# Two attention blocks on one core: GpSimd's shifts over four blocks instead of three, the third score bank lent at any time, and a semaphore that holds GpSimd back behind VectorE's shifts and copies of V

## The chip, the cores and the metric

One core of a Trainium2 chip runs the whole program. The metric is device time in microseconds (us), and less is better. Of the engines, TensorE is called PE, VectorE DVE, ScalarE ACT, GpSimd POOL and SyncE SP, as in the profile. PE does matrix products into PSUM (eight banks of 128 partitions by 512 float32 each), ACT does exponentials, DVE and GpSimd do elementwise work, SP issues DMAs.

## The reference, cut to what matters

Both halves have one input of 2048 rows and 512 columns, 32 heads of width 16, and an output projection. Half A is linear attention (cheap); half B is full softmax attention, which is nearly all of the work.

```python
    def _A_ref(x, wqkv, wo):
        ...
        phi = lambda t: jnp.where(t > 0, t + 1, jnp.exp(t)) + 1e-6
        pq, pk = phi(q), phi(k)
        kv = jnp.einsum("bhsd,bhse->bhde", pk, v)
        ...
    def _B_ref(x, wqkv, wo):
        ...
        scores = jnp.einsum("bhqd,bhkd->bhqk", q, k) * scale
        p = _softmax(scores, axis=-1)
        o = jnp.einsum("bhqk,bhkd->bhqd", p, v)
        return (lambda x, *d: x.transpose(*d))(o, 0, 2, 1, 3).reshape(B, S, D) @ wo
```

The two results stand side by side in the output, 2048 by 1024.

## The kernel before

**The unit of work is a block**: 128 keys by 512 queries of one head. There are 32 units (head groups, query stretches and the even or odd heads of a group), each of 64 blocks for four heads, 2048 blocks in all. Each block is one matmul of K and Q into one PSUM bank (`qk`, L863), an exponential, and one or more matmuls of the exponentials with V that add into the bank `pPV` (L1224). V carries a column of ones, so the same product gives the softmax's denominator.

**The exponential is made in one of two ways.** On the ACT way, PE fills two or three banks of the tile `pS` and ACT takes the exponential of all of them in one instruction into `PT` (L1095). `pS` has two slots, of three and two banks (`ABL = (3, 2)`), filled in turn; each further bank makes an instruction longer, and there are fewer of them. On the D way, DVE turns a bank of scores into 16-bit integers that, read as float16, are a coarse exponential (tile `DI`, L970). To make it finer, the same integers are shifted by a constant twice (tile `DJ`, L1166, `k` of 1 and 2), and PE multiplies all three with three copies of V of different weights (`VV`, `k` of 0, 1, 2). So a block of the D way costs DVE one pass over PSUM, GpSimd two shifts, and PE three products with V instead of one. The shifts are done for a group of `DG = 3` blocks at a time, 1536 columns, two instructions to a group, into one of `NDJ = 8` buffers. They run on GpSimd; where GpSimd's planned backlog is over `LM` beyond DVE's, one goes to DVE.

**What sets the order.** A planner in Python runs when the program is built. It keeps a planned time for each engine (`T`), a list of candidates with durations and priorities, and always takes the one that can start first. The order in which it takes them becomes each engine's fixed instruction stream; `Sched.add` notes for each instruction what it must wait for by semaphore. No engine can deviate from this order on the chip. `fill_act_cand` fills a slot of `pS` and, on the way, up to two D blocks into free D banks (`d_pick`); `fill_d_cand` fills a D block alone; `shift_cand` places a shift; `pv_cand` places the products with V; `job_cand` places the projections, half A and the V copies. How many blocks go each way is not set by a number: it falls out of how soon ACT, DVE and GpSimd are free in the plan.

**Banks.** PSUM holds five banks of `pS`, one of `pPV`, two of `pD` (the D banks). The third bank of the large slot can be lent to the D way: then ACT's instruction of that slot takes two banks. `want_lend` decides it; before the change it is lent mainly while a projection or a half A job holds one of the D banks.

**V copies.** For the first head group, DVE itself makes the weighted copies of V (`v4_job`, eight instructions of 544 columns); later ones are made by GpSimd.

**End.** In the last unit no D block is begun once fewer than `DEND = 12` blocks are left; then follow the last exponentials (split in two halves), the last products with V, the division by the denominator, the output projection and the last stores.

The names above are local functions of one large function. Here are those that the change touches:

## Time and profile before

| | |
|---|---|
| time, median of 3 runs | 683.81 us (683.69 to 686.09) |
| the profiled execution | 684.12 us, of which the span of its instructions is 682.4 us |
| PE busy | 653.9 us (96%) |
| ACT busy | 669.0 us (98%) |
| GpSimd (POOL) busy | 622.1 us (91%) |
| DVE busy | 582.6 us (85%) |
| granted clock of TensorE, mean | 0.997 |

The busy time of PE is a poor guide, because its matmuls are pipelined, their ends are modelled, and an instruction that waits with its weights loaded hides in the row of the weight loads. The share of ACT and GpSimd can be taken nearer to the letter, apart from one point: ACT's and DVE's instructions overlap by a few tenths of a microsecond, so that the mean duration of one is longer than the distance between the starts of two. Where a rate matters, it is taken from start to start.

### The profile page before, as it was taken

The page shows a single profiled execution, that of the slowest core. Times are in us where ns is not written, and L with a number is a line of the kernel's source. Part 1 is how long each engine was busy: PE and PEld are TensorE (multiplying, and loading weights), DVE is VectorE, ACT ScalarE, POOL GpSimd, SP SyncE. Part 2 cuts the span into 40 slices and gives each one's busy share as a digit, 9 for nine tenths or more (in the row PEclk, how much of TensorE's full clock was granted, in tenths as well). Part 3 has the DMA queues.
Part 4 walks back from the last instruction along what each step waited for, and adds up shares of the span by engine and source line. Part 5 has one row for each costly group of instructions (what it writes and reads, how often), then busy time and mean ns, then how long its engine had stood idle before and what let it go on. Part 6 is the DMA issues. An engine that isn't in the chain of part 4 may idle for free.

```text
span 682.4 us, 19594 instructions
## 1 busy us (share of the span) xinstructions
PE 653.9 (96%) x8530; PEld 209.9 (31%) x8530; DVE 582.6 (85%) x937; ACT 669.0 (98%) x706; POOL 622.1 (91%) x470
## 2 busy tenths in 40 slices
PE   8999999999999999999999999999999999999997
PEld 4323333222323333332322233222332222322223
DVE  5878898999789988868999898888888998898983
ACT  5999999999999999999999999999999999999997
POOL 6698999999699999999999999999999999999894
PEclk9999999999999999999999998999999999999999
DMA  9400012011101201130111000111010110001111
GB/s 207 103 2 2 17 16 35 10 31 23 34 2 33 33 17 17 22 82 11 24 25 33 24 18 18 24 47 25 18 36 13 33 32 25 9 17 33 47 41 35
DMA packets 55418, 21.76 MB, mean 32 GB/s; under 512 B 45600, under 2 KB 55328, under 8 KB 55328
## 3 DMA queue, kind: packets, MB, share of 16 engines
q1 hardware_dynamic: 54128, 20.07, 13.4%
q8 instruction: 68, 1.11, 0.7%
q10 hardware_dynamic: 1200, 0.39, 0.2%
q14 instruction: 22, 0.18, 0.1%
HBM read 4.19 MB, written 4.19 MB: 12 GB/s over the span
## 4 chain that ended last, share of the span: by engine, by line
ACT 87%; POOL 7%; PE 3%; DVE 2%; DMA 1%; issue 0%; ACTq 0%
ACT PT L1095 85%; POOL DJ L1166 6%; ACT pD L683 1%; DVE DI L970 1%; PE pS L863 1%; DMA xTb<-in_B_x_dram 1%; ACT pS L683 1%; PE pD L535 1%; PE pPV L1224 1%; PE pS L535 1%; PE pS L654 0%; POOL XN L1359 0%; ACT KV L539 0%; POOL VV L671 0%; DVE DJ L1166 0%
## 5 line engine op out<-in xcount | busy, mean ns | idle before, releaser
L1095 ACT ACTIVATE PT<-pS 128x1024 f16<-128x1024 f32 (+1 forms) x666 | 660.5, 1353 | 2.6 <-PE pS L863 1.8
L1166 POOL TENSOR_SCALAR DJ<-DI 128x1536 int16<-128x1536 int16 (+1 forms) x391 | 579.5, 1483 | 48.0 <-DVE DI L970 21.6
L970 DVE TENSOR_SCALAR DI<-pD 128x512 uint16<-128x512 f32 (+1 forms) x456 | 315.2, 705 | 48.4 <-PE pD L863 42.8
L863 PE MATMUL pS<-QT,KM 32*128 32x512 bf16 x1573 | 261.5, 385 | 21.3 <-ACT PT L1095 15.0
L1224 PE MATMUL pPV<-PT,VV 128*17 128x512 f16 (+1 forms) x1420 | 244.0, 378 | 0.5 <-DVE OT L1354 0.5
L1224 PE MATMUL pPV<-DJ,VV 128*17 128x512 f16 (+1 forms) x1256 | 231.9, 379 | 0.7 <-POOL DJ L1166 0.5
L863 PE MATMUL pD<-QT,KM 32*128 32x512 bf16 x475 | 168.5, 385 | 0.3 <-DVE PQT L684 0.3
L863 PEld LDWEIGHTS pS<-QT,KM 32*128 32x128 bf16 x1573 | 64.3, 91 | 278.0 <-ACT PT L1095 260.3
L1224 PE MATMUL pPV<-DI,VV 128*17 128x512 f16 (+1 forms) x628 | 148.3, 379 | 0.5 <-DVE OT L1354 0.4
L970 DVE TENSOR_SCALAR DI<-pS 128x512 uint16<-128x512 f32 x153 | 104.1, 681 | 8.0 <-PE pS L863 4.4
L1224 PEld LDWEIGHTS pPV<-PT,VV 128*17 128x17 bf16 x1420 | 49.8, 88 | 44.0 <-issue 38.1
L1224 PEld LDWEIGHTS pPV<-DJ,VV 128*17 128x17 bf16 x1256 | 47.9, 88 | 47.2 <-issue 35.6
L863 PEld LDWEIGHTS pD<-QT,KM 32*128 32x128 bf16 x475 | 39.7, 91 | 9.3 <-issue 4.1
L1224 PEld LDWEIGHTS pPV<-DI,VV 128*17 128x17 bf16 x628 | 31.2, 88 | 22.4 <-issue 18.4
L1166 DVE TENSOR_SCALAR DJ<-DI 128x1536 int16<-128x1536 int16 x29 | 28.3, 977 | 0.0
L535 PE MATMUL pD<-xTb,Wb 128*32 128x512 bf16 (+1 forms) x368 | 26.7, 379 | 0.0
L535 PE MATMUL pD<-Wa,xTa 128*32 128x256 bf16 x672 | 26.4, 275 | 0.0
L1354 DVE STREAM_TRANSPOSE OT<-pPV 128x512 f32<-128x512 f32 x31 | 22.0, 708 | 0.7 <-PE pPV L1224 0.6
L1359 POOL TENSOR_TENSOR XN<-OT,ZRA 128x256 bf16<-128x256 f32 x31 | 19.5, 630 | 1.2
L683 ACT ACTIVATE pD<-pD 128x512 f32<-128x512 f32 x22 | 19.6, 893 | 0.0
L671 POOL TENSOR_SCALAR VV<-VV 128x544 bf16<-128x544 bf16 x24 | 17.3, 723 | 0.9
L535 PEld LDWEIGHTS pD<-Wa,xTa 128*32 128x32 bf16 x672 | 15.4, 96 | 8.7 <-issue 5.4
(109 smaller groups left out, 392.3 us busy)
## 6 DMA issues: line engine op xcount, KB each, us to landing
out_dram<-KV SPq DMA_DIRECT2D x31, 128.0 KB, 1.7
Wa<-in_A_wqkv_dram SPq DMA_DIRECT2D x3, 512.0 KB, 4.2
KM<-KR SPq DMA_DIRECT2D x96, 16.0 KB, 1.8
Wb<-in_B_wqkv_dram SPq DMA_DIRECT2D x2, 384.0 KB, 4.6
Wb<-in_B_wqkv_dram SPq DMA_DIRECT2D x1, 512.0 KB, 4.4
Wa<-in_A_wo_dram SPq DMA_DIRECT2D x1, 512.0 KB, 4.5
Wb<-in_B_wo_dram SPq DMA_DIRECT2D x1, 512.0 KB, 3.8
xTa<-in_A_x_dram SPq DMA_TRANSPOSE x24, 3.4
```

Of the source, the lines that this page charges most:

```text
L535: ins = e.matmul(out[32 * g:32 * g + 32], lhsT=lhsT[:, 32 * g:32 * g + 32], rhs=rhs, start=start, stop=stop, tile_position=(0, 32 * g))
L671: st.append((lane, 0.74 if lane == "dve" else VVT, f_op(lane, lambda e, k=k: e.tensor_scalar(vv(k), vv(0), SW[k], 0.0, op0=ALU.mult, op1=A ...
L683: ex = lambda bk: sch.add("act", lambda e: e.activation(x(bk), x(bk), ACTF.Exp), reads=[bk[3]], writes=[bk[3]])
L863: return e.matmul(dst, lhsT=KM[32 * g:32 * g + 32, Gp % 2, e_, j * 128:(j + 1) * 128], rhs=QT[32 * g:32 * g + 32, Gp % 2, c * 512:(c + 1) ...
L970: sch.add("dve", lambda e: e.tensor_scalar(DI.bitcast(U16)[:, buf, i * 512:(i + n) * 512], f32v(DBANK[bi], 512 * n), EB, IMAX, op0=ALU.add ...
L1095: sch.add("act", lambda e: e.activation(PT[:, row, c0:c0 + w], SCR[sl][:, 0:w], ACTF.Exp, scale=SC / ESC), reads=skeys(sl)[:len(bl)], writ ...
L1166: sch.add(ln, lambda e: e.tensor_scalar(J, I, 1.0, float(SH[k]), op0=ALU.mult, op1=ALU.add), reads=[("DI", buf, i) for i in range(n)], wri ...
L1224: sch.add("pe", lambda e: e.matmul(dst[32 * g:32 * g + 17, 0:n], lhsT=VV[:, Gp % 2, k, j, 17 * h:17 * h + 17], rhs=P[:, q0:q0 + n], start= ...
L1354: sch.add("dve", lambda e: e.transpose(OT[:, 0, :], PVb[:, 0:512]), reads=[("PV", g) for g in range(4)], writes=[("OT", 0)])
L1359: mul = f_op("pool" if XNP else "dve", lambda e: e.tensor_tensor(xn[:, :, 16 * e_:16 * e_ + 16], o[:, :, 0:16], zr.unsqueeze(2).broadcast_ ...
```

## The change

Seven edits go together, and since the planner sets the order, every engine's stream is a new one.

1. A group has four blocks instead of three (`DG` 4, four buffers of `DI` instead of six, six of `DJ` instead of eight), so a shift is 2048 columns wide.
2. A shift or a copy of V that DVE makes is put on a list `hold`, and the next instruction given to GpSimd waits for it. The plan has DVE wait for the end of GpSimd's planned instruction first, prices the shift itself at 0.45 and the copy at 0.27 in place of 0.40 + 0.0003 a column and 0.74, and puts GpSimd's time behind it.
3. The third bank is lent whenever no D bank is free and neither DVE's nor GpSimd's planned backlog is over a bound (`want_lend`), and with a third bank on loan a D bank that a job holds keeps it lent.
4. Numbers that were one for the whole run (how early a D block is filled, when products with V get precedence, GpSimd's allowed backlog, and two more) are now chosen by stretches of 45 us of the plan from five sets (`MODES`), by the seeds that also shift the due times of the projections and of half A.
5. A job whose last step was GpSimd's counts as ready 0.8 later (`JM`); `PVW` goes from 0.3 to 0; the planner's weights for how busy PE is are changed.
6. The first projections are made by matmuls of 128 columns of weights instead of four of 32 (`first_units`).
7. The plan's start times are changed by up to 0.25, GpSimd's from 16.0 to 8.4.

```diff
+        if lane == "pool" and self.hold:
+            extra_deps = list(extra_deps) + self.hold
+            self.hold = []
...
-    DG = 3
-    NDG = 6
-    NDJ = 8
+    DG = 4
+    NDG = 4
+    NDJ = 6
...
+    MODES = ((0.8, 36, 0.7, 0.2, 9.0), (1.2, 36, 0.7, 0.2, 9.0), (0.8, 48, 0.9, 0.2, 10.5), (1.2, 28, 0.7, 0.1, 9.0), (1.0, 36, 0.55, 0.35, 8.0))
...
+    DSH = 0.45
...
-                        ins = mm4(e, bk[0][:, bk[2] + o0:bk[2] + o0 + n], Wb[:, cc, kind * 512:kind * 512 + 128], xTb[:, cc, c0:c0 + n], cc == 0, cc == 3)
+                        ins = e.matmul(bk[0][:, bk[2]:bk[2] + n], lhsT=Wb[:, cc, kind * 512:kind * 512 + 128], rhs=xTb[:, cc, c0:c0 + n], start=(cc == 0), stop=(cc == 3))
...
+                if lane == "dve":
+                    def alone(bk, cp=cp):
+                        sch.hold.append(cp(bk))
+                        sch.hold[-1].x = 0.27
+                    alone.kind = "x"
+                    st.append(("dve", 0.27, alone))
+                else:
+                    st.append((lane, VVT, cp))
...
         def want_lend(t_):
             nh = sum(1 for i in range(ND) if held.get(i))
-            if LD == 3:
+            if LD == 1:
                 return nh >= 1
-            if LD == 4:
-                return nh >= 2
-            if d_backlog(t_) > LB:
+            free = sum(1 for x in dfree if x is not None and x <= t_ + 0.1)
+            if LD == 2 and sum(1 for i in range(len(dfree)) if held.get(i)) > sum(lent):
+                return True
+            if free:
                 return False
...
-            return False
+            return d_backlog(t_) <= LB and p_backlog(t_) <= PB5
...
-            dp, dd = POOLT(w), 0.40 + w * 0.0003
             sp, sd = max(T["pool"], vis("dve", t_), jfree[jb]), max(T["dve"], t_, jfree[jb])
+            dp, dd = POOLT(w), DSH + max(0.0, T["pool"] - sd)
...
+                if ln == "dve":
+                    T["pool"] = max(T["pool"], vis("dve", en_))
...
+                op = sch.add(ln, lambda e: e.tensor_scalar(J, I, 1.0, float(SH[k]), op0=ALU.mult, op1=ALU.add),
+                             reads=[("DI", buf, i) for i in range(n)], writes=[("DJ", jb)])
+                if ln == "dve":
+                    sch.hold.append(op)
+                    op.x = DSH
```

What the new plan contains, counted in the two programs:

| | before | after |
|---|---|---|
| ACT, exponentials of two banks (1024 columns) | 579 | 581 |
| ACT, exponentials of three banks (1536) | 86 | 78 |
| ACT, exponentials of one bank (512) | 1 | 0 |
| ACT, the two last ones, columns each | 768 | 512 |
| blocks by the ACT way | 1420 | 1398 |
| blocks by the D way | 628 | 650 |
| DVE, `DI` of one bank / of two banks | 590 / 19 | 626 / 12 |
| GpSimd, full shifts | 389 of 1536 | 288 of 2048 |
| GpSimd, short shifts | 2 of 512 | 2 of 1024 |
| DVE, shifts | 29 of 1536 | 36 of 2048 |
| GpSimd's shifts that wait for a semaphore of PE | 27 | 92 |

**ACT, from its first exponential on.** `PT<-pS` of 1024 columns takes two banks of scores, of 1536 three. Before:

```order
L571 ACTIVATE QT<-pD 128x256
L1095 ACTIVATE PT<-pS 128x1024 x14
L1095 ACTIVATE PT<-pS 128x1536
L1095 ACTIVATE PT<-pS 128x1024
L1095 ACTIVATE PT<-pS 128x1536
```

And now:

```order
L580 ACTIVATE QT<-pD 128x256
L1111 ACTIVATE PT<-pS 128x1024 x6
L1111 ACTIVATE PT<-pS 128x1536
L1111 ACTIVATE PT<-pS 128x1024 x21
L1111 ACTIVATE PT<-pS 128x1536
L1111 ACTIVATE PT<-pS 128x1024 x3
```

Before, runs in which the two widths alternate (bank not lent) stand beside runs of 1024 (bank lent); now runs of 1024 are broken by single ones of 1536.

**GpSimd, between its 16th and 17th multiplication by the reciprocals** (`XN<-OT,ZRA`, one a unit, so this is the middle of the run). `s_dve` and `s_pe` are the semaphores that DVE and PE raise. Before:

```order
L1359 TENSOR_TENSOR XN<-OT,ZRA 128x16x16 [waits s_dve]
L1166 TENSOR_SCALAR DJ<-DI 128x1536 x2
L1166 TENSOR_SCALAR DJ<-DI 128x1536 [waits s_dve] x2
L1166 TENSOR_SCALAR DJ<-DI 128x1536
L1166 TENSOR_SCALAR DJ<-DI 128x1536 [waits s_dve]
```

And now:

```order
L1379 TENSOR_TENSOR XN<-OT,ZRA 128x16x16 [waits s_dve]
L1184 TENSOR_SCALAR DJ<-DI 128x2048 [waits s_pe] x2
L1184 TENSOR_SCALAR DJ<-DI 128x2048 [waits s_dve]
L1184 TENSOR_SCALAR DJ<-DI 128x2048 [waits s_pe]
L1184 TENSOR_SCALAR DJ<-DI 128x2048 [waits s_dve]
```

The shifts are wider, and those whose input was ready anyway now wait for PE to give back the `DJ` buffer, of which there are six instead of eight.

**DVE and GpSimd, their last shifts.** Before, DVE's last pass over scores is followed by the transposes of the final normalization, and GpSimd ends with ordinary pairs:

```order
L970 TENSOR_SCALAR DI<-pS 128x512 [waits s_pe]
L970 TENSOR_SCALAR DI<-pD 128x512 [waits s_pe] x2
L1288 STREAM_TRANSPOSE OT<-pPV 128x256 [waits s_pe]
L1289 RECIPROCAL ZRA<-OT 128x8 [waits s_dve]
L1288 STREAM_TRANSPOSE OT<-pD 128x256 [waits s_pe]
```

Now DVE (the first fence) makes a last shift, and GpSimd (the second) has two full ones, of which the second is held until DVE's is done, and a group of two blocks:

```order
L988 TENSOR_SCALAR DI<-pS 128x512 [waits s_pe]
L988 TENSOR_SCALAR DI<-pD 128x512 [waits s_pe]
L1184 TENSOR_SCALAR DJ<-DI 128x2048
L1309 STREAM_TRANSPOSE OT<-pPV 128x256 [waits s_pe]
L1309 STREAM_TRANSPOSE OT<-pD 128x256 [waits s_pe]
```

```order
L1184 TENSOR_SCALAR DJ<-DI 128x2048 [waits s_pe]
L1184 TENSOR_SCALAR DJ<-DI 128x2048 [waits s_dve]
L1184 TENSOR_SCALAR DJ<-DI 128x1024
L1184 TENSOR_SCALAR DJ<-DI 128x1024 [waits s_pe]
L1311 TENSOR_TENSOR XN<-OT,ZRA 128x8x16 [waits s_dve]
```

Behind DVE's last pass over scores there are now one shift of DVE and three of GpSimd, of which two are short.

More of the change, by code (lines that the diff above doesn't have):

```diff
@@ L1049, in fill_act_cand @@
             start = max(T["pe"], t0, afree[sl], ptfree.get((row, sl), 0.0) - 0.5)
[L1050 to L1051 removed]
+            if sl in LIX and wd == 3 and lent[sl]:
+                start = max(start, dfree[LIX[sl]])
             dur = switch("q") + 0.22
[L1053 removed]
+            late = T["act"] + sum(exps) - dur - TAIL["pe"] - SEM - mode()[3]
             if nfill[0] >= NS and start < late:
@@ L1317, in ahead_cand @@
         def ahead_cand():
-            assert cur_unit() is not None or not lent[0]
             if cur_unit() is not None or not ahead:
```

110 lines of the change are left out of this document (54 added, 56 removed).

## The prediction

> **What bounds the kernel now.** I read the busy times and the chain of the page first, then the groups of instructions with shapes kept apart, then who waits for whom, and last the timeline.
>
> ```profile
> PE 653.9 (96%) x8530; PEld 209.9 (31%) x8530; DVE 582.6 (85%) x937; ACT 669.0 (98%) x706; POOL 622.1 (91%) x470
> ACT 87%; POOL 7%; PE 3%; DVE 2%; DMA 1%; issue 0%; ACTq 0%
> ```
>
> ACT carries 87% of the chain that ended last. The groups (line, engine, operation, tiles, shapes, count, busy us, mean ns, idle before them) say with what:
>
> ```profile
> L1166 POOL TENSOR_SCALAR DJ<-DI 128x1536 int16<-128x1536 int16 x389 | 578.2, 1488 | 47.8 <-DVE DI L970 21.6
> L1095 ACT ACTIVATE PT<-pS 128x1024 f16<-128x1024 f32 x579 | 574.9, 1299 | 2.6 <-PE pS L863 1.8 <-PE pD L863 0.8
> L970 DVE TENSOR_SCALAR DI<-pD 128x512 uint16<-128x512 f32 x437 | 292.1, 683 | 44.5 <-PE pD L863 38.9 <-PE pS L863 2.2
> ...
> L1095 ACT ACTIVATE PT<-pS 128x1536 f16<-128x1536 f32 x86 | 148.2, 1723 | 0.0
> L1166 DVE TENSOR_SCALAR DJ<-DI 128x1536 int16<-128x1536 int16 x29 | 28.3, 977 | 0.0
> L970 DVE TENSOR_SCALAR DI<-pD 128x1024 uint16<-128x1024 f32 x19 | 23.1, 1217 | 3.9 <-PE pD L863 3.9
> L1359 POOL TENSOR_TENSOR XN<-OT,ZRA 128x256 bf16<-128x256 f32 x31 | 19.5, 630 | 1.2
> L671 POOL TENSOR_SCALAR VV<-VV 128x544 bf16<-128x544 bf16 x24 | 17.3, 723 | 0.9
> L1095 ACT ACTIVATE PT<-pS 128x512 f16<-128x512 f32 x1 | 0.9, 878 | 0.0
> L1166 POOL TENSOR_SCALAR DJ<-DI 128x512 int16<-128x512 int16 x2 | 1.2, 618 | 0.2
> ```
>
> All 666 exponentials together waited 2.6 us: ACT is fed without a gap, so its time is its work. PE is not the limit although it reads 96%:
>
> ```profile
> PEld pS L863 <- ACT PT L1095: 260.3, 588, 1.4
> DVE DI L970 <- PE pD L863: 46.1, 99, 2.0
> PEld pPV L1224 <- POOL DJ L1166: 7.5, 26, 0.8
> ```
>
> PE's weight loads for the scores wait 260.3 us for ACT to give a slot back, 0.44 us each of 588 times; for GpSimd's shifts PE waits 7.5 us in all. GpSimd is the second limit, because its shifts decide how many blocks ACT is spared. Its rate, ACT's rate, and both ends of the run from the timeline (start, us, engine, what, count):
>
> ```profile
> 8.83 1.02 ACT L1095 ACTIVATE PT<-pS 128x1024 f16<-128x1024 f32 x1 [1.00 <-PE pS L863]
> 531.98 38.12 ACT L1095 ACTIVATE PT<-pS 128x1024 f16<-128x1024 f32 x41
> 674.48 1.51 ACT L1016 ACTIVATE PT<-pS 128x768 f16<-128x768 f32 x2
> 13.13 6.11 POOL L1166 TENSOR_SCALAR DJ<-DI 128x1536 int16<-128x1536 int16 x4 [5.03 <-DVE DI L970]
> 40.47 12.32 POOL L1166 TENSOR_SCALAR DJ<-DI 128x1536 int16<-128x1536 int16 x8
> 669.89 3.02 POOL L1166 TENSOR_SCALAR DJ<-DI 128x1536 int16<-128x1536 int16 x2 [0.21 <-DVE DI L970]
> ```
>
> Two-bank exponentials start (38.12 - 1.30) / 40 = 0.92 us apart; the 1.30 is the last one's whole duration. GpSimd's shifts start (12.32 - 1.47) / 7 = 1.55 us apart, of which 1.47 (a single one, quoted below) is the shift and 0.08 the step to the next. 389 of them are 603 us. With the two short ones (1.4), 24 copies of V at 0.72 + 0.08 (19.3) and 31 multiplications at 0.63 + 0.08 (22) that is 646 us, between 8.1 (where the wait of 5.03 begins) and 672.9, which is 664.8 us. GpSimd is full, too.
>
> **ACT's term.** A third bank lengthens an exponential by 1.723 - 1.299 = 0.424 us, 0.83 ns a column, so three-bank ones take 0.92 + 0.424 = 1.344 from start to start. By the counts of the two programs there are 2 more of two banks (+1.84), 8 fewer of three (-10.75), the single one of one bank goes (0.92 - 0.424 = 0.50 less), and the two last ones are 256 columns shorter (2 x 0.21 = 0.42 less). Half A's 32 exponentials stay. Sum: 1.84 - 10.75 - 0.50 - 0.42 = **-9.83 us**. All of it lies on the path, as long as ACT stays fed. That the bank is lent more often is in it: per block, 0.92 / 2 = 0.46 stands against 1.344 / 3 = 0.45, so wider or narrower is worth little; what counts is that 22 blocks leave ACT.
>
> **What the 22 blocks cost elsewhere, GpSimd first.** A full shift is now 2048 columns. From 512 to 1536 columns the duration goes from 0.62 to 1.47, 0.83 ns a column; so I put 1.47 + 0.43 = 1.90 for it, 1.98 from start to start. A block's shift falls from 1.55 / 3 = 0.517 to 1.98 / 4 = 0.495. 288 of them are 570.2, the two of 1024 columns 2.3, the copies and multiplications 41.3 as before: 613.8 us. If nothing else moved, GpSimd could work from 8.1 to 663.1, which leaves 655 - 613.8 = 41 us. Out of these come the new waits.
>
> **The wait behind VectorE.** Before, GpSimd was held already, without a semaphore. DVE's shift at 317.16, and GpSimd's before and after it:
>
> ```profile
> 317.16 1.60 DVE L1166 TENSOR_SCALAR DJ<-DI 128x1536 int16<-128x1536 int16 x1
> ...
> 316.87 1.47 POOL L1166 TENSOR_SCALAR DJ<-DI 128x1536 int16<-128x1536 int16 x1
> ...
> 318.31 1.77 POOL L1166 TENSOR_SCALAR DJ<-DI 128x1536 int16<-128x1536 int16 x1
> ...
> 432.40 0.54 DVE L1166 TENSOR_SCALAR DJ<-DI 128x1536 int16<-128x1536 int16 x1
> ...
> 19.93 0.29 DVE L671 TENSOR_SCALAR VV<-VV 128x544 bf16<-128x544 bf16 x1
> ```
>
> DVE's shift ended at 318.76, 0.42 us after GpSimd's shift (318.34): it had stood until GpSimd was done. GpSimd's next one took 1.77 instead of 1.47. So each DVE shift cost GpSimd 0.30 us and DVE up to a whole shift of GpSimd. With GpSimd out of its way, DVE's took 0.54. The slope from the free copy of 544 columns to it is 0.25 ns a column, so 2048 columns take 0.67 free, or 0.42 + 0.13 = 0.55 behind GpSimd's end.
>
> With the semaphore, GpSimd starts 0.55 + 0.08 behind its own end, where the 0.08 is what it took at 669.89 to follow a pass of DVE that ended at 669.81:
>
> ```profile
> 669.12 0.69 DVE L970 TENSOR_SCALAR DI<-pD 128x512 uint16<-128x512 f32 x1 [1.62 <-PE pD L863]
> ```
>
> Without a hold it would start 0.08 behind. It loses 0.55 a shift, then, instead of 0.30. For 36 shifts that is 20 us, for the 8 copies some 2 (0.29 each): 22 of the 41. The other end of this cost is rival A. Queued behind the held instruction is every later shift, and for those PE's products with V wait, and behind these PE's next scores.
>
> [...]
>
> **DVE.** It gets 36 passes of one bank more (292.1 / 437 = 0.668 each, 24.0) and 7 of two banks fewer (1.22 each, 8.5): +15.5. Its 36 shifts cost 0.67 each at the least and 1.90 + 0.55 = 2.45 at the most, depending on where in GpSimd's shift they come. I take the middle of GpSimd's shift, 0.95 + 0.55 = 1.5: 54 instead of 28.3, so +25.7. DVE then works 624 of 673 us; with the two ends, 594 to 658. Its idle time, 682.4 - 582.6 = 99.8, halves to 49, and is 15 at the worst. I price this at 0 with a remainder: the cover is PE's 0.44 us of reserve at each slot, and the stall of 1.60 us at 317.16 did no harm. Without this cover each such stall would be ACT's.
>
> **Smaller parts.** GpSimd waits for PE on 92 shifts instead of 27; before, no row of waits shows GpSimd waiting for PE, so I take 0 for these. The 16-to-4 matmuls at the start (first exponential at 8.83 now) I take as 0, within 0.3 either way, since they work the same columns. At the end there are new steps: DVE's last pass ended at 669.81, 6.2 us before ACT's last exponential (676.0). Behind it come now a rest of a GpSimd shift (0 to 1.98), DVE's 0.55, GpSimd's 1.98 and two of 1.13: 4.8 to 6.8 instead of 3.1. That ends between 1.4 before and 0.6 behind ACT's end, plus the products; I take +0.3, within 0 and 1.
>
> **Sum.** -9.83 + 0.3 = -9.5. To this I add 0.7 for feeding ACT from a DVE with half the reserve: from -2.6 (all waits gone) to +7.2 (rival B). The profiled execution took 684.12, the median of the three runs is 683.81; from the former, 684.12 - 9.83 + 0.3 + 0.7 = **675.3**.
>
> **The rivals.**
> *A, slower: the hold idles GpSimd.* GpSimd now waits until DVE reaches its shift. [...] There are 44 holds and 41 us: from 0.93 us a hold GpSimd becomes the bound, and from 0.93 + 9.8 / 44 = 1.15 the kernel is slower than before. At 1.5 us it takes 675.3 + 66 - 41 = 700. For it speaks that DVE's spare time halves; against it, that a shift is given to DVE only when GpSimd is far behind, so that GpSimd is at work when DVE comes.
> *B, no change: DVE's stalls reach ACT.* If each of 36 shifts costs ACT 0.2 us more, by a D bank that is freed late and scores queued behind it on PE, 7.2 of the 9.8 are given back: 682. Against it speaks the stall at 317.16, for it the thinner reserve.
> *C, the clock.* The granted clock fell once (a window of the run: its bounds and length, busy time of PE, its weight loads, DVE, ACT and GpSimd, the granted clock, DMA):
>
> ```profile
> 360.00:420.00 60.00, 58.04 (x713) 18.93 (x705) 54.05 (x86) 59.34 (x65) 57.10 (x42) 0.97 0.11 26
> ...
> 418.94 1.02 ACT L1095 ACTIVATE PT<-pS 128x1024 f16<-128x1024 f32 x1 [0.37 <-PE pD L863]
> 420.41 2.86 ACT L1095 ACTIVATE PT<-pS 128x1024 f16<-128x1024 f32 x3 [0.45 <-PE pD L863]
> ```
>
> These two gaps cost ACT 0.8 us. Five more such drops make 679. [...]
> *D, the wide shift is no cheaper per block.* At 0.517 a block, 2048 columns take 2.07, GpSimd 26 us more; with 22 for the holds 7 are missing: 682.
>
> **How the numbers follow.** My forecast, 673 to 678.5, has 0.64; C 0.05; B 0.13; D 0.04; A 0.14. B and D lie mostly within 0.5% (680.4 to 687.2 from 683.8), which is about what a measurement of this kernel can tell from no change. So faster 0.70 (forecast, C, a little of B), same 0.16, slower 0.14. The predicted time is the forecast's. The range starts where all of ACT's 2.6 us of waits are gone, 671.7, rounded to 672, and goes up to include C and most of B and D, 683.5; A is left out.
>
> **What would show it.** Right: 581 and 78 exponentials at 0.92 and 1.34 from start to start, still with some 3 us of idle time before them; GpSimd's full shift at 1.90, 1.98 from start to start; behind a DVE shift GpSimd starts some 0.63 after its own end. Wrong: PE's weight loads for the scores wait for DVE or GpSimd instead of ACT, and the idle time before the exponentials is over 8 us (B); GpSimd's idle time before shifts, released by DVE, is over 41 us (A); a granted clock clearly below 0.997 (C); a shift of over 1.98 us (D).

## The result, and the profile after

The changed kernel takes **677.93 us** (median of 4 runs, 676.98 to 678.51); the kernel before takes 683.75 beside it. The ratio is 0.9902, with a 95% interval of 0.9885 to 0.992: faster by 1%. A second measurement on another occasion gave 0.9913 (0.9894 to 0.9931). The forecast was 675.3, so the direction and most of the size came out, and 2.6 us are missing. The profiled execution took 678.51 us, with a span of 676.8.

The page's busy times and the chain that ended last, after:

```profile
PE 645.3 (95%) x8533; PEld 207.6 (31%) x8533; DVE 593.4 (88%) x973; ACT 659.0 (97%) x699; POOL 590.5 (87%) x369
ACT 92%; PE 5%; DVE 1%; DMA 1%; issue 0%; ACTq 0%
```

GpSimd is out of the chain, where it had 7%, and ACT has 92%. The groups with shapes kept apart (line, engine, operation, tiles, shapes, count, busy us, mean ns, idle before them):

```profile
L1111 ACT ACTIVATE PT<-pS 128x1024 f16<-128x1024 f32 x581 | 568.7, 1279 | 4.0 <-PE pD L881 2.1 <-PE pS L881 1.8
L1184 POOL TENSOR_SCALAR DJ<-DI 128x2048 int16<-128x2048 int16 x288 | 547.4, 1901 | 70.0 <-DVE DJ L1184 30.0 <-DVE DI L988 18.7 <-DVE VV L681 2.1
L988 DVE TENSOR_SCALAR DI<-pD 128x512 uint16<-128x512 f32 x469 | 311.7, 682 | 34.3 <-PE pD L881 27.3 <-PE pS L881 4.0
...
L1111 ACT ACTIVATE PT<-pS 128x1536 f16<-128x1536 f32 x78 | 130.6, 1674 | 0.1
...
L1184 DVE TENSOR_SCALAR DJ<-DI 128x2048 int16<-128x2048 int16 x36 | 29.3, 815 | 0.0
```

ACT's exponentials still wait for next to nothing, 4.1 us in all. GpSimd now stands idle for 70.0 us ahead of its shifts, 30.0 of them behind the semaphore. DVE's shift of 2048 columns takes 0.815 us on average; the one of 1536 took 0.977. The waits, in the same form as before (who, for whom, us in all, times, longest):

```profile
PEld pS L881 <- ACT PT L1111: 238.3, 529, 1.0
...
DVE DI L988 <- PE pD L881: 30.2, 83, 1.4
POOL DJ L1184 <- DVE DJ L1184: 30.0, 31, 3.0
```

PE still has a reserve of 0.45 us (238.3 / 529) at a slot of scores, so ACT sets the pace as before. GpSimd waits 0.97 us (30.0 / 31) for each shift of DVE that it waits for at all.

The span falls by 5.6 us. Cut at ACT's first and last exponential in the two traces, it reads:

| | before | after | difference |
|---|---|---|---|
| start of the first exponential | 8.83 | 9.06 | +0.23 |
| from there to the end of the last exponential | 667.16 | 658.22 | -8.94 |
| from there to the end of ACT's last copy | 3.75 | 5.00 | +1.25 |
| from there to the landing of the last store | 2.13 | 3.99 | +1.86 |
| from there to the end | 0.50 | 0.50 | 0 |

The middle gained what was forecast; the tail lost 3.1 us of it again. So there are two things to test: what made the middle shorter (the counts, the semaphore, the wide shift), and what made the tail longer. Edits 5, 6 and 7 (`JM`, `PVW` and the weights for PE, the first projections, the start times of the plan) were not taken apart.

### The profile page after: what moved, and what is told of

Same layout as the page of the kernel before. It is cut to its first block, busy times and chain, and to the rows that moved or that the text cites. A ratio compares the mean times of both kernels' runs of the same rounds, so it can differ in the third digit from the quotient of the medians.

```text
span 676.8 us, 19573 instructions
## 1 busy us (share of the span) xinstructions
PE 645.3 (95%) x8533; PEld 207.6 (31%) x8533; DVE 593.4 (88%) x973; ACT 659.0 (97%) x699; POOL 590.5 (87%) x369
## 3 DMA queue, kind: packets, MB, share of 16 engines
HBM read 4.19 MB, written 4.19 MB: 12 GB/s over the span
## 4 chain that ended last, share of the span: by engine, by line
ACT 92%; PE 5%; DVE 1%; DMA 1%; issue 0%; ACTq 0%
ACT PT L1111 90%; ACT pD L701 2%; PE pS L881 2%; PE pPV L1245 1%; DMA xTb<-in_B_x_dram 1%; ACT pS L701 1%; PE pS L544 1%; PE pD L544 0%; PE pD L751 0%; PE pD L664 0%; DVE DI L988 0%; PE pS L573 0%; DVE OT L1309 0%; PE pD L573 0%; ACT KV L548 0%
## 5 line engine op out<-in xcount | busy, mean ns | idle before, releaser
L1111 ACT ACTIVATE PT<-pS 128x1024 f16<-128x1024 f32 (+1 forms) x659 | 649.2, 1326 | 4.1 <-PE pD L881 2.1
L1184 POOL TENSOR_SCALAR DJ<-DI 128x2048 int16<-128x2048 int16 x290 | 549.5, 1895 | 70.2 <-DVE DJ L1184 30.0
L988 DVE TENSOR_SCALAR DI<-pD 128x512 uint16<-128x512 f32 (+1 forms) x481 | 326.2, 695 | 36.5 <-PE pD L881 29.3
L1245 PE MATMUL pPV<-PT,VV 128*17 128x512 f16 (+1 forms) x1398 | 228.4, 379 | 0.0
L1245 PE MATMUL pPV<-DJ,VV 128*17 128x512 f16 (+1 forms) x1300 | 222.4, 379 | 0.0
L881 PE MATMUL pD<-QT,KM 32*128 32x512 bf16 x493 | 177.9, 385 | 0.2
L881 PEld LDWEIGHTS pS<-QT,KM 32*128 32x128 bf16 x1555 | 64.3, 91 | 276.6 <-ACT PT L1111 238.3
L1245 PEld LDWEIGHTS pPV<-PT,VV 128*17 128x17 bf16 x1398 | 46.3, 88 | 40.6 <-issue 35.9
L1184 DVE TENSOR_SCALAR DJ<-DI 128x2048 int16<-128x2048 int16 x36 | 29.3, 815 | 0.0
L544 PE MATMUL pD<-xTb,Wb 128*32 128x512 bf16 x304 | 23.3, 383 | 0.0
L548 DVE CAST KV<-pD 128x512 bf16<-128x512 f32 x21 | 14.4, 686 | 5.8 <-PE pD L544 5.8
L701 ACT ACTIVATE pD<-pD 128x512 f32<-128x512 f32 x23 | 19.1, 829 | 0.3 <-DVE PQT L700 0.3
```

The costliest lines, as they stand in the source:

```text
L544: ins = e.matmul(out[32 * g:32 * g + 32], lhsT=lhsT[:, 32 * g:32 * g + 32], rhs=rhs, start=start, stop=stop, tile_position=(0, 32 * g))
L548: return lambda e, bk: (e.tensor_copy(out_fn(), in_fn(bk)) if lane == "dve" else e.activation(out_fn(), in_fn(bk), ACTF.Copy))
L701: ex = lambda bk: sch.add("act", lambda e: e.activation(x(bk), x(bk), ACTF.Exp), reads=[bk[3]], writes=[bk[3]])
L881: return e.matmul(dst, lhsT=KM[32 * g:32 * g + 32, Gp % 2, e_, j * 128:(j + 1) * 128], rhs=QT[32 * g:32 * g + 32, Gp % 2, c * 512:(c + 1) ...
L988: sch.add("dve", lambda e: e.tensor_scalar(DI.bitcast(U16)[:, buf, i * 512:(i + n) * 512], f32v(DBANK[bi], 512 * n), EB, IMAX, op0=ALU.add ...
L1111: sch.add("act", lambda e: e.activation(PT[:, row, c0:c0 + w], SCR[sl][:, 0:w], ACTF.Exp, scale=SC / ESC), reads=skeys(sl)[:len(bl)], writ ...
```

## Experiments on the middle

### The semaphore alone taken out

The plan, the order and the counts stay; only the wait of GpSimd goes.

```diff
         if lane == "pool" and self.hold:
-            extra_deps = list(extra_deps) + self.hold
             self.hold = []
```

> The same order and the same counts as after, but GpSimd's next instruction no longer waits for VectorE's shift or copy. [...] Theory HOLD (the semaphore is what keeps VectorE from standing behind a whole shift of GpSimd, and VectorE's delays reach ACT): VectorE's shift over 1.3 us on average, ACT's idle time over 7 us, time 681 or more.

Measured: 685.22 us (10 runs, 682.88 to 691.37), ratio 1.0007 (0.9979 to 1.0034). All of the gain is gone: 7.3 us by the two medians, 6.4 against the kernel before, which took 684.68 beside this run and beside the runs with groups of three, without the lending and without the seeds, and 683.75 beside the changed kernel. A comparison of medians across these two occasions is good to about 1 us. The groups of this kernel:

```profile
L1110 ACT ACTIVATE PT<-pS 128x1024 f16<-128x1024 f32 x581 | 563.4, 1226 | 10.6 <-PE pD L880 5.2 <-PE pS L880 5.1
L1183 POOL TENSOR_SCALAR DJ<-DI 128x2048 int16<-128x2048 int16 x288 | 557.1, 1936 | 62.9 <-DVE DI L987 33.7 <-PE pPV L1244 11.6 <-DVE RHA L754 0.6
...
L1183 DVE TENSOR_SCALAR DJ<-DI 128x2048 int16<-128x2048 int16 x36 | 40.6, 1128 | 0.0
```

DVE's 36 shifts take 11.3 us more than with the semaphore, GpSimd's 288 take 9.7 us more, and ACT's idle time grows from 4.0 to 10.6. One place shows how. DVE's shift, GpSimd's shifts beside it and the next transposition on DVE, without the semaphore (timeline: start, us, engine, line, operation, tiles, count, idle before):

```profile
99.93 4.19 POOL L1183 TENSOR_SCALAR DJ<-DI 128x2048 int16<-128x2048 int16 x2
...
100.44 1.93 DVE L1183 TENSOR_SCALAR DJ<-DI 128x2048 int16<-128x2048 int16 x1
...
102.89 0.70 DVE L1373 STREAM_TRANSPOSE OT<-pPV 128x512 f32<-128x512 f32 x1
...
103.65 0.40 PE L1244 MATMUL pPV<-DI,VV 128*17 128x512 f16 x4 [0.23 <-DVE OT L1373]
...
104.73 1.02 ACT L1110 ACTIVATE PT<-pS 128x1024 f16<-128x1024 f32 x1 [0.84 <-PE pS L880]
```

And the same shift with it, in the changed kernel:

```profile
100.46 0.68 DVE L1184 TENSOR_SCALAR DJ<-DI 128x2048 int16<-128x2048 int16 x1
...
101.23 3.88 POOL L1184 TENSOR_SCALAR DJ<-DI 128x2048 int16<-128x2048 int16 x2 [1.23 <-DVE DJ L1184]
101.66 0.70 DVE L1374 STREAM_TRANSPOSE OT<-pPV 128x512 f32<-128x512 f32 x1
```

The shift arrives at the same point of the program. Without the semaphore GpSimd has begun its next shift 0.51 us earlier, and DVE's takes 1.93 instead of 0.68. The transposition that frees the bank for the products with V comes 1.23 later, PE's products wait for it, and ACT stands for 0.84 us. What follows is told by the windows (bounds, length, busy time and count of PE, its weight loads, DVE, ACT and GpSimd, granted clock, DMA), first without the semaphore, then with it:

```profile
100.00:104.00 4.00, 2.51 (x25) 0.58 (x21) 4.00 (x5) 3.89 (x5) 3.92 (x2) 1.00 0.09 23
104.00:108.00 4.00, 4.00 (x41) 0.66 (x33) 3.03 (x7) 2.30 (x3) 2.52 (x3) 0.57 0.00 0
```

```profile
100.00:104.00 4.00, 3.27 (x39) 0.73 (x35) 4.00 (x7) 4.00 (x6) 2.69 (x3) 1.00 0.09 24
104.00:108.00 4.00, 4.00 (x52) 0.96 (x56) 3.86 (x7) 4.00 (x5) 3.60 (x3) 1.00 0.01 4
```

PE was busy for 2.51 of 4 us instead of 3.27, and in the next 4 us the granted clock is 0.57 and ACT works 2.30 us instead of 4.00. So what ACT loses here in the stretch with the clock at 0.57, 1.70 us (4.00 - 2.30), is more than the 0.84 that it stands at first. That the stall of DVE brings the fall of the clock about is not shown, and not every stall has one behind it: after the one at 596.43 (a DVE shift of 2.40 us, then an exponential that is late by 1.5 us) the clock stays full, although PE was busy for only 2.02 of these 3.41 us:

```profile
595.89:599.30 3.41, 2.02 (x18) 0.52 (x13) 3.41 (x3) 3.41 (x4) 3.33 (x3) 1.00 0.00 0
```

Call an exponential late if it starts over 0.15 us later behind the one before than the median for that one's width (only where ACT does nothing else between the two). Without the semaphore 22 are late, by 14.4 us in all; in the changed kernel 7, by 4.3. Of the 14.4, seven that follow within about 4 us of a DVE shift of over 1.5 us (there are nine such; in the changed kernel one) make 6.4, and the others inside the two stretches of half clock (104.3 to 107.7, 503.7 to 513.9) 4.4. The ten runs agree: at a mean granted clock of 0.997 six runs took 682.9 to 685.4, at 0.994 one took 684.5, at 0.987 two took 687.4 and 687.5, at 0.982 one took 691.4. HOLD holds, then; the mean of DVE's shift, 1.13, is below the 1.3 that HOLD expected, because 27 of the 36 shifts still come when GpSimd is idle or in the second half of its instruction.

### The semaphore put into the kernel before

The other half of the same question: is it good by itself?

```diff
+        if lane == "pool" and self.hold:
+            extra_deps = list(extra_deps) + self.hold
+            self.hold = []
...
-                sch.add(ln, lambda e: e.tensor_scalar(J, I, 1.0, float(SH[k]), op0=ALU.mult, op1=ALU.add),
-                        reads=[("DI", buf, i) for i in range(n)], writes=[("DJ", jb)])
+                op = sch.add(ln, lambda e: e.tensor_scalar(J, I, 1.0, float(SH[k]), op0=ALU.mult, op1=ALU.add),
+                             reads=[("DI", buf, i) for i in range(n)], writes=[("DJ", jb)])
+                if ln == "dve":
+                    sch.hold.append(op)
```

(The expectation speaks of 8 copies of V as well; the kernel that ran holds GpSimd for the 29 shifts alone.)

> The kernel before, in its own order, with the semaphore alone: GpSimd's next instruction waits for each of DVE's 29 shifts and 8 copies of V. Theory PLAN: the semaphore is worth what DVE's stalls cost ACT, and in the plan of before they cost nothing (ACT idle 2.6 us in all), so the time stays within 1.5 us of before, 682.5 to 685.5, although DVE's shift falls from 0.98 to about 0.75 on average. [...]

Measured: 686.72 us (12 runs, 684.97 to 687.51), ratio 1.0034 (1.0023 to 1.0045): slower by 2.9 us and above the 682.5 to 685.5 that PLAN expected. Two of its groups:

```profile
L1170 POOL TENSOR_SCALAR DJ<-DI 128x1536 int16<-128x1536 int16 x389 | 573.6, 1475 | 55.1 <-DVE DI L974 20.8 <-DVE DJ L1170 8.5
...
L1170 DVE TENSOR_SCALAR DJ<-DI 128x1536 int16<-128x1536 int16 x29 | 31.4, 1084 | 0.0
```

DVE's shift didn't become shorter but longer, 1.084 instead of 0.977: seven of the 29 now take over 1.5 us instead of two, and all seven come in the first quarter of a GpSimd shift. In its profile 1.9 us come from a later start (first exponential at 10.74 instead of 8.83; that the semaphore brings this about isn't shown, see the section on the two ends), and 1.2 from the middle (668.38 instead of 667.16), where 24 exponentials are late by 7.4 us, against 8 by 3.5 before. PLAN was right that there is nothing to win, and missed that GpSimd, held at places that the plan didn't know of, costs something (1.2 us by this profile). The semaphore and the plan that counts on it belong together: each alone brings nothing or less.

### Groups of three in the changed kernel

```diff
-    DG = 4
-    NDG = 4
-    NDJ = 6
+    DG = 3
+    NDG = 6
+    NDJ = 8
```

> Everything of the change, but groups of three blocks (1536 columns), six DI and eight DJ buffers as before. The plan has 562 exponentials of two banks and 96 of three (after: 581 and 78), 53 shifts on VectorE (36). Theory COUNT (time is ACT's work, so the sum of its exponentials sets it): -19 x 0.915 + 18 x 1.341 + 0.42 = +7.2 us against after, 685. Theory SUPPLY (what counts is that GpSimd's work fits; 369 x 1.55 = 572 us here and 288 x 1.98 = 570 in after are the same): within 1.5 us of 677.9.

Measured: 685.11 us (10 runs, 684.53 to 687.93), ratio 1.002 (1.0003 to 1.0036). The plan now has 562 exponentials of two banks and 96 of three; the count's +7.2 on 677.93 is 685.1. That the medians meet to the tenth is in part luck (against the kernel before beside each, the difference is 6.2); the better test is the time between first and last exponential, 664.3 in its profile, against 657.1 to 657.2 in six profiles of the changed kernel's middle without a stretch of half clock: +7.1. This middle is still 2.9 shorter than the one before the change; a tail that is 3.1 longer (9.47 against 6.38 behind the last exponential) makes the two kernels about equal.

```profile
L1184 POOL TENSOR_SCALAR DJ<-DI 128x1536 int16<-128x1536 int16 x369 | 543.8, 1474 | 79.7 <-DVE DJ L1184 38.7 <-DVE DI L988 13.0 <-DVE VV L681 3.1
...
L1184 DVE TENSOR_SCALAR DJ<-DI 128x1536 int16<-128x1536 int16 x53 | 32.9, 628 | 0.0
```

53 shifts on DVE cost GpSimd 38.7 us of holding instead of 30.0. What is lost shows nowhere as a wait of ACT: it lies in the number of blocks that the plan leaves to ACT, 1415 instead of 1398.

### Groups of four in the kernel before

```diff
-    DG = 3
-    NDG = 6
-    NDJ = 8
+    DG = 4
+    NDG = 4
+    NDJ = 6
```

> The kernel before with the first edit alone: groups of four blocks, shifts of 2048 columns (DG 4, NDG 4, NDJ 6). Its plan has 520 exponentials of two banks and 138 of three, DVE 12 shifts. Theory COUNT (time follows what the plan leaves to ACT, 0.915 us for two banks and 1.341 for three): -59 x 0.915 + 52 x 1.341 - 0.5 = +15.2, 699.0. Theory WIDE (the wide shift is the gain, being cheaper a block): faster than before, 675 to 682.

Measured: 705.39 us (4 runs, 705.17 to 706.46), ratio 1.0306 (1.0278 to 1.0333). Three of its groups:

```profile
L1166 POOL TENSOR_SCALAR DJ<-DI 128x2048 int16<-128x2048 int16 x282 | 538.8, 1911 | 102.2 <-DVE DI L970 85.1
...
L1095 ACT ACTIVATE PT<-pS 128x1536 f16<-128x1536 f32 x138 | 232.1, 1682 | 0.1
...
L1166 DVE TENSOR_SCALAR DJ<-DI 128x2048 int16<-128x2048 int16 x12 | 16.6, 1382 | 0.0
```

WIDE falls: the same cheap shift (1.911 us for four blocks) makes the kernel before slower by 3%. GpSimd stands idle for 102.2 us, because DVE, in the old plan, doesn't deliver the blocks (85.1 of it), and 52 more exponentials take three banks. Of the +20.5 the count gives 15.2; the rest shows in the profile as 18 late exponentials of 8.8 us (8 of 3.5 before), with half clock at 12.7, 142.4 to 149.2 and 364.2, and in a tail 2.3 us longer. The middle alone grows by 19.1.

### The lending and the seeds

Two more parts undone, one at a time, in the changed kernel: the bank lent only while a job holds a D bank, and all seeds zero (one set of numbers for the whole run, and no shifted due times).

```diff
-    LD = 2
+    LD = 1
```

> Everything of the change, but the third bank is lent only while a job holds a D bank. The plan has 527 exponentials of two banks, 122 of three and one of one bank, 17 shifts on VectorE. Theory COUNT: -54 x 0.915 + 44 x 1.341 + 0.5 + 0.42 = +10.5 us against after, 688.4. Theory WIDTH (per bank a three-bank exponential is a little cheaper, 0.447 against 0.458 us, and ACT has as many columns to do as the D way leaves it, so lending is worth nothing or less): within 1.5 us of 677.9 or faster.

```diff
-    SEEDS = (0, 357, 103, 277, 20, 42, 55, 76, 197, 262, 78, 81, 233, 301, 371)
+    SEEDS = (0,) * 15
```

> Everything of the change, but all seeds are 0: the first set of MODES everywhere, no shift of due times. The plan has 550 exponentials of two banks and 108 of three, 20 shifts on VectorE. Theory COUNT: -31 x 0.915 + 30 x 1.341 + 0.42 = +12.3 us against after, 690.2, slower than before, although every mechanism of the change is in it. Rival SEEDS-DON'T-MATTER (they only shift when small jobs are due): within 1.5 us of 677.9.

Measured: 692.22 us (4 runs, 691.65 to 693.81), ratio 1.0113 (1.0083 to 1.0143), without the lending; 689.94 us (6 runs, 687.55 to 692.4), ratio 1.0084 (1.0057 to 1.0112), without the seeds. The groups of exponentials, first of the one, then of the other:

```profile
L1111 ACT ACTIVATE PT<-pS 128x1024 f16<-128x1024 f32 x527 | 538.6, 1281 | 5.2 <-PE pS L881 3.9 <-PE pD L881 1.3
L1111 ACT ACTIVATE PT<-pS 128x1536 f16<-128x1536 f32 x122 | 206.0, 1689 | 1.0 <-PE pD L881 0.9
```

```profile
L1111 ACT ACTIVATE PT<-pS 128x1024 f16<-128x1024 f32 x550 | 554.7, 1307 | 3.8 <-PE pS L881 3.0 <-PE pD L881 0.8
L1111 ACT ACTIVATE PT<-pS 128x1536 f16<-128x1536 f32 x108 | 185.4, 1716 | 0.0
```

The seeds' median is what the count said (690.2), but in part by luck: in its profile the middle is 10.9 longer than in the six profiles, 1.4 less than the count, and the start is 2.1 later. The lending's is 3.8 us above the count (688.4), with four stretches of half clock in the middle (12.6 longer), a later start and a longer tail in its profile. Without either, the changed kernel is slower than the kernel before. Each of groups, lending and seeds is worth 6 to 14 us in the changed plan, and the whole change gains 5.8 on the old one: the parts don't add. A likely reason, argued and not shown, is that each takes from the same pool of blocks that leave ACT.

## Experiments on the two ends

The first reading of the tail was that DVE's branch at the program's end (each engine compares a flag and skips a second program) stands for 3.5 us because the code behind it isn't loaded; PE, ACT and DVE are told of the branch 60 instructions ahead (`HINT`). The changed kernel ran once more as a control, and with this mark elsewhere.

```diff
-    HINT = 60
+    HINT = 24
```

> The changed kernel once more, beside the next three. Both theories of the tail expect 677.9 (676.9 to 678.6), and at the end of the profile again a branch of DVE that goes on only 3.4 us later, with the last two stores landing 4.0 us behind the last copy of ACT.

> The same instructions in the same order; only the mark from which PE, ACT and DVE are told of the branch at the end stands 24 instructions ahead of it instead of 60. Theory FETCH: the tail's excess comes from a branch at the end whose target isn't loaded yet (DVE's took 3.4 us, and the stores issued beside the loading landed 4 us late instead of 2). With the mark elsewhere, other engines or none find their code missing: if no branch takes over 1 us, the stores land about 2.1 us behind the last copy and the time falls by 1.9 to 676.0; if a branch of another engine takes 3 us, the time stays at 677.9. Theory STORE: the last two stores are slow for a reason of their own (their order, their queue): they land 4 us behind the last copy whatever the branches do, 677.9.

And with `HINT = 120`:

> The same with the mark 120 instructions ahead. FETCH: as for 24, that is 676.0 if no branch takes over 1 us, 677.9 if one of DVE or ACT does. STORE: 677.9 either way.

Measured: 678.7 us as it is (5 runs, 677.3 to 679.21; 0.1 above the range that was expected), 677.85 with 24 (4 runs, 677.57 to 679.53), 677.96 with 120 (5 runs, 676.76 to 679.28). No difference beyond the spread of the runs. With 120 DVE's branch no longer stands (0.63 us instead of 2.9 to 3.5), and the stores are as slow as before. So the first form of FETCH falls. The row of what the DMA engines moved, for the tail alone (40 equal slices, GB/s), shows what is slow. Before, from 678.7 to 683; after, from 671.5 to 677, with the issues of the last two stores and their median time to landing:

```profile
GB/s 0 0 0 0 0 0 0 0 76 352 324 334 124 200 362 333 248 143 295 343 352 324 334 334 315 86 0 0 0 76 229 76 0 0 0 0 0 0 0 0
```

```profile
GB/s 119 350 343 357 335 313 90 0 179 313 276 82 298 350 224 30 127 7 22 30 37 22 67 7 30 7 7 15 22 22 22 7 0 60 0 0 0 0 0 0
...
out_dram<-KV SPq DMA_DIRECT2D x2, 128.0 KB, 4.1
```

Before, the stores run mostly at 300 GB/s and more to their end, and a short burst (76, 229, 76) stands behind them: packets of instructions. After, the stores are nearly through just as fast, and then a trail of 7 to 67 GB/s drags on for 2 us, which is the last few packets of the last two stores. In the trace four packets of instructions (8 and 16 KB, up to 1.0 us each) start at 673.2 to 674.6, among those of the stores; before, four (up to 1.3 us) started at 681.9 to 682.1, behind them. In both they come 1.2 us or more behind the first branch, so what differs is the order of branch and stores: before, the last store was issued at 679.77 and the first branch taken at 680.70; after, the branch came at 671.67 and the last two stores at 671.81 and 672.29.

The test of this puts the branch behind the landing:

```diff
+            if queue != "pool":
+                for s_ in last.values():
+                    e.wait_ge(sems[s_.lane], s_.count * 16)
             with e.If(got[0] > FLAG_BITS):
```

> The changed kernel; only, PE, ACT, DVE and SP wait until the last stores have landed before they take the branch at the program's end (GpSimd does so anyway). Theory FETCH, second form: what slows the last two stores (3.4 to 4.1 us in four profiles) is the loading of instructions that starts about 1 us behind the first branch, whether or not a branch stalls; before the change all four stores were issued ahead of the first branch. With the branch behind the stores, the last store lands about 2.1 us behind the last copy, as before the change. If no engine then stalls at its branch, the end comes 0.5 to 1.0 later and the time falls by 0.8 to 1.8; if one stalls for 1.5 to 3 us, the gain is eaten up. Theory STORE: the last two stores take 3.4 to 4.1 us all the same, and the time stays at 678 or grows by 0.3.

Measured: 679.09 us (6 runs, 678.46 to 680.36), ratio 0.9922 (0.9901 to 0.9943). The same row of this kernel, from 670.5 to 678:

```profile
GB/s 0 197 371 333 333 164 5 311 317 153 339 262 11 0 0 0 44 0 0 0 0 87 87 0 0 0 0 0 0 0 0 0 0 0 0 0 0 0 44 0
...
out_dram<-KV SPq DMA_DIRECT2D x2, 128.0 KB, 1.7
```

The trail is gone, the two stores land after 1.7 us instead of 4.1, 1.73 behind the last copy instead of 3.99. STORE falls. But DVE's branch now stands for 3.6 us at the very end, where nothing covers it, and the gain is eaten up: the kernel before took 684.87 beside it, and 5.8 less is what the changed kernel gained, too. The mark that had no effect alone should take that away.

The start is the other end. With 36 idle products of PE ahead of the first projections, these come in two speeds, 1.91 and 1.04 us for eight of them. That 44 idle products bring the faster one was my guess. The control, and then the kernel with 44 of them:

```profile
6.78 1.91 PE L573 MATMUL pD<-xTb,Wb 128*128 128x256 bf16 x8
...
10.94 1.02 ACT L1111 ACTIVATE PT<-pS 128x1024 f16<-128x1024 f32 x1 [2.68 <-PE pS L881]
```

```profile
7.05 1.04 PE L573 MATMUL pD<-xTb,Wb 128*128 128x256 bf16 x8
...
9.64 1.02 ACT L1111 ACTIVATE PT<-pS 128x1024 f16<-128x1024 f32 x1 [1.57 <-PE pS L881]
```

```diff
-            for i_ in range(36):
+            for i_ in range(44):
```

> The changed kernel with 44 instead of 36 idle products of PE ahead of the first projections (they multiply a unit matrix and nobody reads the result). In the profiles the first exponential starts either at 8.8 to 9.7 or at 10.7 to 11.4, and in the second case the first projections of 256 columns take 1.91 us instead of 1.04. [...] Theory LOAD: the late start comes from the landing of the input; then the two starts remain, and the time stays at 677.9 to 678.7.

Measured: 677.57 us (6 runs, 676.71 to 678.28), ratio 0.9895 (0.9874 to 0.9915). The median is 0.4 to 1.1 below the changed kernel's two (7.3 below the kernel before beside it, where those are 5.8 and 5.1 below), and the spread is 1.6 (the changed kernel's two have 1.5 and 1.9). Input that lands late is not the reason (it landed at 6.3 in the late start and at 6.8 in the early one), so LOAD falls; that 44 products bring the early start in every run is not shown.

All three edits of the ends together, the mark at 120:

> The changed kernel with three edits of the ends: the branch behind the landing of the stores, 44 idle products at the start, and the mark of the branch 120 instructions ahead (with which no branch took over 0.6 us in the one profile of it). FETCH: the stores land 1.7 us behind the last copy, as in the profile with the branch behind them, and without DVE's stall of 3.6 us the end comes 0.6 later: from the first exponential at 9.6 and the last one's end at 666.8 that is 666.8 + 5.0 + 1.7 + 0.6 = 674.1 for the span, 675.8 for the time, against 677.9 to 678.7 of the changed kernel. If DVE or ACT stalls at its branch again, the span is 676.8 to 677.7 and the time 678.5 to 679.4: then the mark doesn't decide which engine finds its code.

Measured: **676.74 us** (4 runs, 676.12 to 677.11), ratio 0.9897 (0.9881 to 0.9914), where 675.8 was expected; the profile's span is 674.4 where 674.1 was expected. From 670.5 to 675:

```profile
GB/s 0 0 173 355 337 355 364 309 310 128 0 55 291 373 319 128 173 373 355 228 37 0 0 0 0 0 0 0 0 73 0 0 0 0 0 73 0 218 0 0
...
out_dram<-KV SPq DMA_DIRECT2D x2, 128.0 KB, 1.7
```

The ends of all these kernels in figures, from the traces (us; "branch" is the time from DVE's branch to its next instruction):

| | mark | first exponential | last copy behind last exponential | landing behind it | DVE's branch | end behind last exponential |
|---|---|---|---|---|---|---|
| before | 60 | 8.83 | 3.75 | 2.13 | 0.63 | 6.38 |
| after | 60 | 9.06 | 5.00 | 3.99 | 3.47 | 9.49 |
| after, again | 60 | 10.94 | 5.00 | 3.39 | 2.94 | 8.89 |
| mark 24 | 24 | 11.35 | 4.99 | 3.75 | 3.13 | 9.24 |
| mark 120 | 120 | 9.66 | 5.00 | 3.40 | 0.63 | 8.90 |
| branch behind stores | 60 | 9.24 | 5.00 | 1.73 | 3.59 | 10.91 |
| 44 products | 60 | 9.64 | 5.00 | 3.59 | 2.88 | 9.10 |
| all three | 120 | 9.26 | 5.00 | 1.73 | 0.63 | 7.92 |

The last kernel has the lowest median of all that ran, 1.2 us below the changed one's first and 2.0 below its second (the kernel before took 683.75 to 683.77 beside all three). The times don't tell it from the kernel with 44 products: its runs overlap with that one's, and it is 7.0 below the kernel before beside it, where that one is 7.3. So the gain of the tail alone, 1.6 by the table (9.49 - 7.92), rests on the profiles.

## Why the prediction was right, and where it was off

**ACT's term** (-9.83). Right. In the two profiles the middle is 8.94 shorter. Each of them has one stretch of half clock (0.50 for 3.41 us), though; the six profiles of the same middle without one have 657.1 to 657.2, 10.0 below before. Seventeen exponentials of two banks from 454.47 on in the changed kernel (15.82 us to the last one's end) give the pace, (15.82 - 1.28) / 16 = 0.91, against 0.92 put (1.28 is the mean duration of one):

```profile
454.47 15.82 ACT L1111 ACTIVATE PT<-pS 128x1024 f16<-128x1024 f32 x17
```

That the count decides was tested from the other side: with groups of three the middle grew by 7.1 where the count says 7.2, without the seeds by 10.9 (12.3), without the lending by 12.6 (10.5). So the count gives the sign and the size to within 0.1 to 2.1 us.

**GpSimd's rate.** Right: 1.90 us for the wide shift, and 1.98 from start to start, here (9.82 - 1.90) / 4:

```profile
224.06 3.88 POOL L1184 TENSOR_SCALAR DJ<-DI 128x2048 int16<-128x2048 int16 x2 [0.63 <-DVE DJ L1184]
...
479.11 9.82 POOL L1184 TENSOR_SCALAR DJ<-DI 128x2048 int16<-128x2048 int16 x5 [1.08 <-DVE DJ L1184]
```

**The wait behind VectorE** (0.63 a shift, 22 of 41 us). The 0.63 is right where DVE stands ready when GpSimd ends, as at 224.06. The sum was too small: in 14 of the 36 cases DVE begins its shift only after GpSimd has ended, and GpSimd stands for 0.8 to 3.0 us, as at 479.11 for 1.08. It is rival A's mechanism, at 0.97 us a wait instead of 0.63; with 31 waits that is 30 of the 41. That GpSimd isn't the bound is seen from the chain, where it has no share any more.

**What the semaphore is worth.** Here the weighing went wrong, though no term of the sum hung on it. I counted the semaphore as a cost alone, 0.55 us of GpSimd a shift instead of 0.30, or 9 us more for 36. Taking it out costs 6.4 to 7.3 us. What this leaves out is where DVE's shifts come without it: in nine of 36 cases GpSimd was in the first half of its next instruction, and nine of DVE's shifts took 1.55 to 2.44 us (1.93 at 100.44) where the one at 100.46 with the semaphore takes 0.68. The order is what the semaphore gives.

**DVE** (36 shifts at 1.5 us). Too high: 0.815, 29.3 us instead of 54. Where DVE comes late (the 14), GpSimd stands already, and the shift takes 0.67 to 0.69 us; and of the 22 that find GpSimd at work 20 come in the last 0.53 us of its instruction, not in the middle. DVE works 593 us, not 624. The remainder put for feeding ACT (+0.7) fits: 4.1 us of waits instead of 2.6, and 1.0 us by which this profile's middle is above that of the others, in which the clock didn't fall.

**The tail** (+0.3, within 0 and 1). This is the term that was mis-sized: +3.1. The reason that I gave for it didn't come about at all. GpSimd's last shift ended 1.0 us ahead of ACT's last exponential:

```profile
665.22 1.05 POOL L1184 TENSOR_SCALAR DJ<-DI 128x1024 int16<-128x1024 int16 x1
```

I looked at who is late ahead of the last exponential, and not at what stands behind it. There the new plan put the reductions for the flag ahead of the second transposition on DVE, and ACT's own store ahead of its last two copies (+1.25), and the branch ahead of the last two stores, which then ran beside the loading of instructions (+1.86). The second is shown by the kernel with the branch behind the stores (why the stores are slower there is not shown). The first is read from the order in the trace and was not tried. ACT's copies and its store, before and after:

```profile
678.16 0.60 ACT L539 ACTIVATE KV<-pD 128x512 bf16<-128x512 f32 x1 [2.17 <-PE pD L535]
678.66 1.08 ACT L539 ACTIVATE KV<-pS 128x512 bf16<-128x512 f32 x2
```

```profile
670.06 0.60 ACT L548 ACTIVATE KV<-pS 128x512 bf16<-128x512 f32 x1 [2.79 <-PE pS L544]
670.69 0.39 ACTq L1333 DMA_DIRECT2D out_dram<-KV  x1
671.18 0.60 ACT L548 ACTIVATE KV<-pD 128x512 bf16<-128x512 f32 x1 [0.52 <-PE pS L544]
```

Half of the 1.25 lies ahead of the first copy (2.79 - 2.17 = 0.62), the other half between the copies, where the store stands. So the tail took 2.8 us more than put, a little over all that is missing between 675.3 and 677.93.

**The rivals.** A: GpSimd's idle time behind DVE's shifts is 30.0, below 41. To the letter, though, the sign that was put down (idle time before shifts, released by DVE) came up without A coming true: with DVE's passes over scores (18.7) and its copies of V (2.1) it is 50.8. Before the change those passes already stood for 21.6 of it, so the sign was badly put. B: ACT's waits are 4.1, below 8; but B's mechanism is real, and it is what happens when the semaphore is taken out. C: one fall of the clock, at 500.9, 3.41 us long and worth 0.8 us as before. What brings a fall about is not shown; in the 3.41 us ahead of this one PE was busy for 2.91 (and for 2.83 ahead of the fall at 416.8 in the kernel before):

```profile
497.52:500.93 3.41, 2.91 (x41) 1.15 (x37) 3.36 (x7) 3.41 (x5) 1.93 (x2) 1.00 0.02 5
```

D: 1.98, not 2.07. That the start would be the same within 0.3 held in the profile (+0.23), but it has two speeds, and which one a run gets moves the first exponential by 1.9 us or so (9.06 and 10.94 in two profiles of the changed kernel).

## What to carry to other kernels

Where a plan in software fixes the order of two engines that delay each other (here DVE's shift took 1.93 us beside GpSimd's and 0.68 alone), a semaphore that makes the planned order certain can be worth more than it costs, but only in a plan that counts on it: taking it out of this plan lost 6 to 7 us, putting it into the old one gained nothing. On the path of a saturated engine, count what leaves that engine: for four parts undone or done alone, a count of ACT's instructions gave the change of the middle to within 0.1, 1.4, 2.1 and 3.9 us (of 7 to 19), while the lower price of the wide shift alone pointed the wrong way. A reordered program has a new tail: read there what follows the last work of the bounding engine, down to the stores and the branch.

## What the runs showed of the hardware that was not expected

- **Stores beside the loading of instructions land late.** Two stores of 128 KB landed after 4.1 us with packets of instructions among theirs and after 1.7 without.
- **A branch can stand for 3 us.** DVE's branch stood for 2.9 to 3.6 us with the mark 24 or 60 instructions ahead in the changed kernel, and for 0.63 with 120, in both profiles of it. With 60 it took 0.63 in the kernel before, but 4.0 in the same kernel with groups of four; without the lending or the seeds it is ACT's branch that stands (3.8 and 1.6 us) and not DVE's. Why is open.
- **A DVE shift beside a GpSimd shift can take over twice its time.** Without the semaphore nine of 36 took 1.55 to 2.44 us instead of 0.68, and GpSimd's shift beside one grows as well: 4.19 us for two at 99.93, with the semaphore 3.88.
- **The clock fell behind stretches in which PE was mostly busy.** In the 3.41 us ahead of a fall PE was busy for 2.91 us at 500.9 in the changed kernel and for 2.83 at 416.8 in the kernel before; behind a stretch with 2.02 (without the semaphore, at 595.89) it didn't fall. What decides it is open.
- **The start has two speeds.** In nine of the 14 profiles the full clock is recorded from 5.0 to 7.2 us on and the first exponential starts at 8.6 to 9.7; in five from 9.9 to 11.0 on and 10.7 to 11.4. A fall of the clock in the middle lasted 3.41 us (at 500.9 and at 416.8, to 0.50), or two or three times that (142.4 to 149.2 in the kernel before with groups of four, 503.7 to 513.9 without the semaphore). Which start a run gets, and why, is open: both profiles with 44 idle products have the early one (9.64 and 9.26), two of the changed kernel with 36 have one of each (9.06 and 10.94).
